# Last head set of four query chunks moved by DMA into a dense out-projection, gate and up in one bank, and a new order

## The chip, the cores and the metric

One core of one Trainium2 chip runs the whole kernel. The metric is device time in microseconds (us) of one execution; the median of three runs of the kernel before is 820.38 us. TensorE is called PE, VectorE DVE, ScalarE ACT, GpSimd POOL, and SyncE, which issues nearly all DMAs, SP.

## What is computed

A transformer block with modulation on x of 2048 tokens by 640, with 32 heads of 20 columns, and a bilinear gated layer of width 1536. All tensors are bf16.

```python
mod = (_silu(c) @ w_mod).reshape(c.shape[0], 6, 1, -1)      # sa, ca, ga, sb, cb, gb
h = _layernorm(x) * (1 + ca) + sa
qkv = (h @ wqkv).reshape(B, S, 3, H, Dh)                    # q, k, v
p = softmax(einsum('bhqd,bhkd->bhqk', q, k) * Dh ** -0.5)
x = x + ga * (einsum('bhqk,bhkd->bhqd', p, v) @ wo)         # attention
h = _layernorm(x) * (1 + cb) + sb
x = x + gb * (((h @ w_gate) * (h @ w_up)) @ w_down)         # bilinear layer, no activation
```

## The kernel before, in words

**Tiles.** Queries are cut into five chunks (CHUNKS): three of 512 and two of 256. The 32 heads are eight head sets of four; the four heads of a set sit in the four 32-row groups of PE. A chunk and a head set make an item, 40 items in all. An item of 512 queries has 64 units: one unit is one head, one tile of 128 keys and 512 queries, a score tile of 128 x 512 in one PSUM bank. In the chunks of 256 queries one unit holds two key tiles, so those items have 32 units. All items together have 2048 units.

**Scores and exp.** A score matmul (L1396) writes a unit. Most units go to ACT, whose exp (L1432) takes two banks at once (1024 columns) into the buffers PP; from score group HEADG on, every second group has three banks (1536 columns), and G, the pool of PSUM banks for other work, then has one bank less. QUADS gives, for each item, how many quads of four units go to DVE instead: DVE computes the exponential in integer arithmetic, with four L1456 (PSUM to DB, 128 x 512) and one each of L1488, L1496 and L1493 (128 x 2048) into two DSS terms. PV (L1922) multiplies PP or DSS by V and adds up in PSUM bank 7.

**End of an item.** DVE transposes the sums (L1576), takes the reciprocal of the denominators (L1579), POOL multiplies (L1581; DVE for the last item), and DVE transposes back into OcT (L1588). For head sets 0 to 6, SP then moves the 20 rows of each head from OcT to their place in Ocp (L1599), which holds the chunk's attention output, transposed, in five blocks of 128 rows. The eighth head set stays in OcT.

**Suffix of a chunk.** `suffix(ci)` projects out: five matmuls of Ocp with wo, and a sixth of OcT with wo7 (the rows of wo of the last head set, laid out as OcT has them). The fifth block of Ocp and of wo therefore holds 48 rows, and zeros behind them. DVE adds the result to xck (L1666), takes statistics (L1676), normalises (L1683); PE transposes (L1694), DVE or ACT evict with the modulation to h2T (L1699, L1701); gate and up (L1769, L1780) give hprod, the down-projection is added to xck (L1803) and goes out (L1812). In chunks 0 to 3 the suffix runs during the next chunk's exps, packed as four column tiles (line L856, `quarters`); a pack that is late may be cut into two halves. The last chunk's suffix runs after the last exp, with whole matmuls (L852, `full`). Weights of gate and up come by DMA into stg, or stx in the last chunk.

**Order.** The order of every engine is written when the program is built. `Sched` is a planner with assumed durations: each task has an engine, dependencies and a priority, and PE's next work is chosen by `pick_pe` from scores, PV and the other rounds (`pick_x`). `gate(w)` holds back a suffix's rounds until a given score group, from GATE_F; PVMIN, PVMAX, PVTOL, D_RES, K_LEAD and the like steer the choice. STEAL_GAP says when ACT may take an eviction from DVE. `do_fill` puts filler matmuls (L2240, L2242) where PE's recent work is low. On the chip each engine runs its list in order and waits on semaphores, so an instruction that waits holds up all behind it.

```python
pcs = oc_pieces(j) if j < NSET - 1 else []
...
mms.append((C320, f))                                   # five of Ocp with wo
f = qf(320, lambda tl=tl: OcT[:, oc_last[ci]["s"], tl * 128:(tl + 1) * 128],
             lambda hf=hf: wo7[:, 320 * hf:320 * hf + 320], False, True)
```

Of the kernel before, what the change touches and what calls it, by code (L numbers as in the profile page):

```python
# [25 lines left out]
DMA_SLOW = 0.0015  # L26
DMA_LAT = 1700.0
STEAL_END = 66197.894
STEAL_GAP = 19.496
HAM_W = 3413.3  # L30
HAM_MIN = 2550.0

# [395 lines left out]
    return nwait  # L428


CHUNKS = [(0, 512), (512, 512), (1024, 512), (1536, 256), (1792, 256)]
QUADS = [(0, 4, 3, 3, 4, 3, 4, 3), (3, 4, 3, 4, 3, 3, 4, 4), (3, 4, 3, 4, 3, 4, 3, 4), (1, 2, 1, 2, 1, 1, 1, 1), 1]
D_LEAD = 0.384
NB0, NSS = 2, 3
HEADG = 600
EAGER = 7
X_POOL, X_PIECES, POOL_NS = 0, 4, 1.95
X_LAST = 2
X_TAIL = 0
XBACK = 1  # L440
HOLD = 110
PVTOL = 245
XDPRIO = 2.0
TPRIO = 0.75
TAHEAD = 1
GU_ONE = 0
XCONT = 0
T3_POOL = 1
HEAD_OUT = 2
NPS = 4  # L450
TS_4X, TT_2X = 600.0, 1145.0
WM_GATE = 9
WM_NEED = 1.798
K_DIRECT = (0, 1, 2, 3)
Q_DIRECT = 2
K_LEAD = 0.686
K_ALL = (0,)
KD_LEAD = 0.409
DMA_WINDOW = 900000
D_LATE = 16  # L460
D_RES = 79
PVMIN, PVMAX, PVCAP = 3, 9, 14
PV0 = 0
V_PARTS = [[0, 4], [4, 8]]
V_L1 = 0.2
# [7 lines left out]
PREEMPT = 0.0  # L473
PRE_M = 0.3
PV0N = 1
GATE_F = [1.0, 0.869, 0.999, 0.673, 1.0]
FILL_MIN = 4200.0
FILL_HARD = 0.0
FILL_T0, FILL_TH, FILL_MINH = 2300.0, 17000.0, 7500.0
FILL_MODE = 'P'  # L480
# [2 lines left out]
LN_POOL = ()  # L483
LN_ACT = [1, 3, 5, 7]
XFIRST = 0
LN2P = 1.775
NALT = 1
OPFIRST = 0
HT_L = 0.11
V_L = 0.208  # L490
LATE_A = 3
LATE_L = 2.394
LATEQ = (3,)
LATEQ_A = 4
LATEQ_F = 0.672
QUAD_GAIN = 0.597233983857778
NTERM = 2
XHALF = 1
X_LATE = 30.0
X_HALF = 0.0  # L500


def ps_cost(n):
    return n * 1.042 + 67.0
# [6 lines left out]
def build_kernel(nc, A_x, A_wqkv, A_wo, B_x, B_w_gate, B_w_up, B_w_down, c, w_mod, out):  # L511
# [852 lines left out]
    for i, (tc, b) in enumerate(ql):  # L1364
        packed_round("Q", b, tc, 500 + i, int(gstart[1] + LATEQ_A + gpc[1] * LATEQ_F * i / len(ql)), True)

    z_wo = pool(630, lambda e: e.memset(wo_sb[:, KD - 1, :], 0.0), t_xn[1], prio=8)
    z_w7 = pool(630, lambda e: e.memset(wo7[:], 0.0), t_xn[1], prio=8)
    d_wo = [dma("sp", 128 * (KD - 1) * D * 2, lambda e: e.dma_start(wo_sb[:, 0:KD - 1, :], wov[:, 0:KD - 1, :]), [d_wm[3][0]],
            prio=10),  # L1370
            dma("sp", 48 * D * 2, lambda e: e.dma_start(wo_sb[0:48, KD - 1, :], wov[0:48, KD - 1, :]), [z_wo, d_wm[4][0]], prio=10.1)]
    d_w7 = [dma("sp", DH * D * 2, lambda e, s=s: e.dma_start(
        wo7[32 * s + 1:32 * s + 1 + DH, :], wov[48 + DH * s:48 + DH * s + DH, KD - 1, :]), [z_w7, d_wm[4][0]], prio=10.2) for s in range(4)]
    t_wo = []
# [192 lines left out]
    oc_free = {}  # L1567
    oc_last = {}

    def item_end_tasks(it):  # L1570
        ci, j = items[it]
        n = CHUNKS[ci][1]
        nb32 = n // 32
        slot = ci % 2
        cell = {}
        t1 = Task("dve", n * 1.1 + 70, lambda e: e.transpose(OT[:, 0:n], ps[:, BPV, 0:n]), [], prio=0.0, name=f"T1.{it}")  # L1576
        t1.acq = [(sOT, "o", 1)]
        item_info[it]["t1"] = t1
        t2 = dve(155, lambda e: e.reciprocal(invT[:, 0:nb32].unsqueeze(2),  # L1579
                                            OT[:, 0:n].rearrange("p (b c) -> p b c", c=32)[:, :, 0:1]), [t1], prio=1.5)  # L1580
        f3 = lambda e: e.tensor_tensor(  # L1581
            OTn[:, 0:n].rearrange("p (b c) -> p b c", c=32), OT[:, 0:n].rearrange("p (b c) -> p b c", c=32),
            invT[:, 0:nb32].unsqueeze(2).to_broadcast([128, nb32, 32]), ALU.mult)
        if T3_POOL and it < len(items) - 1:
            t3 = pool(n * 2.2 + 200, f3, [t2], prio=0)
        else:
            t3 = dvl(sb_cost(n, 1.04), f3, [t2], prio=1.5)
        t4 = dve(n * 1.1 + 65, lambda e: e.transpose(OcT[:, cell["s"], 0:n], OTn[:, 0:n]), [t3], prio=1.5)  # L1588
        pcs = oc_pieces(j) if j < NSET - 1 else []
        t4.acq = [(sOcT, "s", max(1, len(pcs)))]  # L1590

        def on4(task):
            cell["s"] = task.slots["s"]
            sOT.done(0, task)
        t4.on_start = on4
        dms = []
        for (b5, s, r0, nr, ro) in pcs:
            def f(e, b5=b5, s=s, r0=r0, nr=nr, ro=ro):
                return e.dma_start(Ocp[r0:r0 + nr, slot, b5, 0:n],  # L1599
                                   OcT[32 * s + 1 + ro:32 * s + 1 + ro + nr, cell["s"], 0:n])  # L1600
            dps = [t4] + ([z_oc[slot]] if b5 == KD - 1 else [])
            if ci >= 2:
                dps += oc_free[ci - 2]
            else:
                dps += [x for l in tr_last.values() for x in l]
            t = dma("sp", nr * n * 2, f, dps, prio=2, dur=720.0)
            t.on_start = lambda task: sOcT.done(cell["s"], task)
            dms.append(t)
        oc_ready.setdefault(ci, []).extend(dms)
        if j == NSET - 1:  # L1610
            oc_ready[ci].append(t4)
            oc_last[ci] = cell
        sc.left += 1
        t1.seq = 0
        return t1
# [5 lines left out]
    def suffix(ci):  # L1621
# [31 lines left out]
        for tl in range(ntl):  # L1653
            ev = []
            for hf in range(2):
                mms = []
                for k in range(KD):
                    f = qf(320, lambda k=k, tl=tl: Ocp[:, slot, k, tl * 128:(tl + 1) * 128],
                                 lambda k=k, hf=hf: wo_sb[:, k, 320 * hf:320 * hf + 320], k == 0, False)
                    mms.append((C320, f))  # L1660
                f = qf(320, lambda tl=tl: OcT[:, oc_last[ci]["s"], tl * 128:(tl + 1) * 128],
                             lambda hf=hf: wo7[:, 320 * hf:320 * hf + 320], False, True)
                mms.append((C320, f))

                def after(r, tl=tl, hf=hf):
                    f = lambda e: e.tensor_tensor(xck[:, tl, 320 * hf:320 * hf + 320], ps[:, r.b["b"], 0:320],  # L1666
                                                  xck[:, tl, 320 * hf:320 * hf + 320], ALU.add)
                    return [dve(ps_cost(320), f, [r.last, d_xc], prio=1)]
                r = Round(mms, list(oc_ready[ci]) + t_wo + [d_xc], after, pr(True), gate=gate(KD * 320),
                          name=f"op{ci}.{tl}")  # L1670
                ev.append(r.evac[0])
                op_last.append(r.last)
            t = t0 + tl
            bn = []
            for hf in range(2):
                bn.append(dve(ps_cost(320), lambda e, tl=tl, hf=hf: e.bn_stats(  # L1676
                    st2[:, tl, 6 * hf:6 * hf + 6], xck[:, tl, 320 * hf:320 * hf + 320]), [ev[hf]], prio=LN2P))
            ag = dve(115, lambda e, t=t, tl=tl: e.bn_aggr(mv2[:, t, :], st2[:, tl, :]), bn, prio=LN2P)
            f1 = lambda e, t=t: e.tensor_scalar(sd2[:, t:t + 1], mv2[:, t, 1:2], EPS, None, op0=ALU.add)
            p1 = dve(75, f1, [ag], prio=LN2P) if tail else pool(220, f1, [ag], prio=1)  # L1680
            p2 = pool(570, lambda e, t=t: e.tensor_tensor(rs2[:, t:t + 1], sd2[:, t:t + 1], mhalf[:, 0:1], ALU.pow),
                      [p1], prio=1)
            t_xn2.append(dvl(360, lambda e, t=t, tl=tl: e.tensor_scalar(  # L1683
                xn2[:, tl, :], xck[:, tl, :], mv2[:, t, 0:1], rs2[:, t:t + 1], op0=ALU.subtract, op1=ALU.mult),
                [p2] + first, prio=LN2P))
            x1_done += ev
        oc_free[ci] = op_last[-1:]
        op_last[-1].on_start = lambda task: sOcT.done(oc_last[ci]["s"], task)
        t_h2 = []
        tr_l = []  # L1690
        for k in range(KD):
            mms = []
            for tl in range(ntl):
                f = lambda e, b, tl=tl, k=k: e.transpose(bankh(b)[:, tl * 128:(tl + 1) * 128],  # L1694
                                                         xn2[:, tl, k * 128:(k + 1) * 128], ident[:])
                mms.append((C128, f))

            def after(r, k=k):
                f = lambda e: e.tensor_scalar(h2T[:, k, 0:n], bankh(r.b["b"])[:, 0:n], mcol[:, 3, k:k + 1],  # L1699
                                              mcol[:, 2, k:k + 1], op0=ALU.mult, op1=ALU.add)  # L1700
                fa = lambda e: e.activation(h2T[:, k, 0:n], bankh(r.b["b"])[:, 0:n], AFT.Identity,  # L1701
                                            bias=mcol[:, 2, k:k + 1], scale=mcol[:, 3, k:k + 1])
                return [evac(n, n * .78 + 55, f, fa, [r.last, r_sb.evac[0], r_cb.evac[0]] +
                             (first if alt else bd.get("h2T", []) + kv_last))]
            r = Round(mms, list(t_xn2), after, pr(True), gate=gate(n), name=f"h2T{ci}.{k}")
            t_h2.append(r.evac[0])
            tr_l.append(r.last)
# [313 lines left out]
    def pick_x(t, warm=False):  # L2021
# [3 lines left out]
        if xcur[0] is not None:  # L2025
# [3 lines left out]
                a = cand.acq[0][0].avail()  # L2029
                blocked = a is None or a[0] > t  # L2030
            pre = False
            if blocked and len(xstack) < 1 or PREEMPT > t and len(xstack) < 2:
                for task in rl:
                    if not blocked and task.prio >= cand.prio - PRE_M:
                        break
# [282 lines left out]
```

The softmax here doesn't subtract the row's maximum and nothing guards it: scores larger than these inputs give would overflow.

## Time and profile before

| | |
|---|---|
| median of three runs | 820.38 us (820.32 to 820.39) |
| the profiled execution: span | 818.5 us; its own time is not listed apart |
| median above the span | 1.9 us |
| first exp starts, last exp ends | 16.27 us, 784.61 us |
| ACT, PE, DVE, POOL busy | 776.9, 789.8, 717.9, 75.7 us |
| exps | 691 of 1024 columns, 91 of 1536, one of 512 |
| quads on DVE | 98 |

The page gives, for each engine, its busy time and share of the span, then groups of instructions: line, engine, operation, what it writes and reads, the count, after the first bar the busy time in us and the mean of one in ns, after the second the idle time of the engine just before them and the line that ended it. Records of one engine may overlap, so that count times mean can be above busy time. In order of time a row gives start, length, engine, line, operation, tiles and count, and in brackets the idle time before it with what ended it. PEld is the loading of weights, SPq the issue of a DMA by SP.

### The profile page before, as it was taken

To read this page: it belongs to the slowest core of one execution; us is meant where nothing else is said; L and a number is where in the kernel's file an instruction comes from. 1 tells how busy PE (TensorE), PEld (TensorE's weight loads), DVE (VectorE), ACT (ScalarE), POOL (GpSimd) and SP (SyncE) were. 2 spreads that over 40 slices of the span, in tenths; PEclk is the share of its full clock that TensorE was granted. 3 is DMA by queue.
4 is the path that set the end of the run, shared out by engine and by line. 5 is a ranking of instruction groups with operands and counts; after the bars stand their busy time and mean duration, and the time that the engine had idled before them with its cause. 6 is when DMAs were issued, how large, how long until landed. Compare 5 with 4: busy or idle time off the path is not lost.

```text
span 818.5 us, 29494 instructions
## 1 busy us (share of the span) xinstructions
PE 789.8 (96%) x12785; PEld 312.7 (38%) x12785; DVE 717.9 (88%) x1262; ACT 776.9 (95%) x825; POOL 75.7 (9%) x105
## 2 busy tenths in 40 slices
PE   8999999999999999999999999999899999999998
PEld 4433333322232332333333333243254443554567
DVE  7989999999999999999999999999798876658663
ACT  7889999999999999999999999999999999999941
POOL 3300000000012000000011000000020000011000
DMA  9724211114400222400300222000301237124420
GB/s 295 219 79 101 71 45 36 51 52 133 104 16 24 59 65 58 134 13 21 93 3 5 54 54 54 6 14 23 90 5 22 54 80 138 33 75 102 104 52 17
DMA packets 115902, 54.35 MB, mean 66 GB/s; under 512 B 83771, under 2 KB 115775, under 8 KB 115775
## 3 DMA queue, kind: packets, MB, share of 16 engines
q1 hardware_dynamic: 114847, 51.33, 24.4%
q8 instruction: 101, 1.65, 0.8%
q10 hardware_dynamic: 928, 1.15, 0.4%
q14 instruction: 26, 0.21, 0.1%
HBM read 41.75 MB, written 8.41 MB: 61 GB/s over the span
## 4 chain that ended last, share of the span: by engine, by line
ACT 49%; PE 38%; issue 9%; DVE 4%; POOL 0%; ACTq 0%
ACT PP L1432 49%; PE ps_all L1396 11%; PE ps_all L856 11%; PE ps_all L1922 8%; PE ps_all L852 3%; PE ps_all L1116 1%; PE ps_all L1052 1%; DVE DB L1456 1%; PE ps_all L1013 1%; DVE DSS L1493 0%; PE ps_all L877 0%; DVE DSS L1488 0%; DVE DSS L1496 0%; DVE st L957 0%; PE ps_all L2242 0%
## 5 line engine op out<-in xcount | busy, mean ns | idle before, releaser
L1432 ACT ACTIVATE PP<-ps_all 128x1024 bf16<-128x1024 f32 (+1 forms) x783 | 758.4, 1234 | 6.1 <-PE ps_all L1396 3.5
L1396 PE MATMUL ps_all<-QT,KT 32*128 32x512 bf16 (+1 forms) x2560 | 308.3, 340 | 19.6 <-ACT PP L1432 14.8
L1456 DVE TENSOR_SCALAR DB<-ps_all 128x512 int16<-128x512 f32 x392 | 260.5, 683 | 35.5 <-PE ps_all L1396 33.7
L1396 PEld LDWEIGHTS ps_all<-QT,KT 32*128 32x128 bf16 x2560 | 81.4, 92 | 262.9 <-ACT PP L1432 240.9
L1922 PE MATMUL ps_all<-PP,Vf 128*32 128x512 bf16 (+2 forms) x2096 | 165.6, 343 | 0.3 <-DVE OT L1576 0.3
L1493 DVE TENSOR_TENSOR DSS<-DB,DSS 128x2048 bf16<-128x2048 bf16 x98 | 119.2, 1216 | 0.0
L856 PE MATMUL ps_all<-h2T,stg 128*32 128x512 bf16 (+1 forms) x1804 | 117.2, 338 | 0.9 <-DVE DB L1456 0.6
L1581 POOL TENSOR_TENSOR OTn<-OT,invT 128x512 bf16<-128x512 f32 (+1 forms) x39 | 41.6, 1066 | 617.6 <-DVE invT L1579 611.8
L1922 PEld LDWEIGHTS ps_all<-PP,Vf 128*32 128x32 bf16 (+1 forms) x2096 | 47.3, 94 | 86.1 <-issue 78.8
L1922 PE MATMUL ps_all<-DSS,Vf 128*32 128x512 bf16 (+3 forms) x928 | 76.9, 351 | 0.1
L1488 DVE TENSOR_SCALAR DSS<-DB 128x2048 int16<-128x2048 int16 x98 | 68.0, 694 | 1.0
L1496 DVE TENSOR_SCALAR DSS<-DB 128x2048 int16<-128x2048 int16 x98 | 67.5, 689 | 1.1 <-PE ps_all L1922 1.1
L856 PE MATMUL ps_all<-wd,hprod 128*32 128x320 bf16 (+1 forms) x1384 | 58.8, 278 | 0.3 <-DVE xck L1803 0.3
L856 PEld LDWEIGHTS ps_all<-h2T,stg 128*32 128x32 bf16 x1804 | 40.7, 96 | 35.0 <-issue 18.1
L856 PEld LDWEIGHTS ps_all<-wd,hprod 128*32 128x32 bf16 x1384 | 31.5, 96 | 17.7 <-issue 9.1
L1769 DVE CAST gsb<-ps_all 128x512 bf16<-128x512 f32 (+1 forms) x48 | 29.6, 618 | 5.1 <-PE ps_all L856 4.8
L1576 DVE STREAM_TRANSPOSE OT<-ps_all 128x512 f32<-128x512 f32 (+1 forms) x40 | 24.2, 605 | 10.2 <-PE ps_all L1922 10.1
L1922 PEld LDWEIGHTS ps_all<-DSS,Vf 128*32 128x32 bf16 (+1 forms) x928 | 23.5, 95 | 23.4 <-issue 9.1
L1116 PE MATMUL ps_all<-hT,wq 128*32 128x512 bf16 x375 | 31.7, 382 | 0.0
L856 PE MATMUL ps_all<-wV,hT 128*32 128x320 bf16 (+1 forms) x688 | 31.2, 292 | 0.0
L856 PE MATMUL ps_all<-wo,Ocp 128*32 128x320 bf16 (+1 forms) x632 | 30.2, 285 | 0.3 <-DVE xck L1666 0.2
L1780 DVE TENSOR_TENSOR hprod<-ps_all,gsb 128x512 bf16<-128x512 f32 x36 | 24.6, 683 | 2.9 <-PE ps_all L856 2.9
(123 smaller groups left out, 532.9 us busy)
## 6 DMA issues: line engine op xcount, KB each, us to landing
stg<-in_B_w_gate_dram SPq DMA_DIRECT2D x50, 160.0 KB
stg<-in_B_w_up_dram SPq DMA_DIRECT2D x50, 160.0 KB
QT<-q_rows SPq DMA_DIRECT2D x22, 128.0 KB
KT<-k_rows SPq DMA_DIRECT2D x84, 32.0 KB
wm<-in_w_mod_dram SPq DMA_DIRECT2D x3, 800.0 KB
x<-in_A_x_dram SPq DMA_DIRECT2D x7, 320.0 KB
xck<-in_A_x_dram SPq DMA_DIRECT2D x3, 640.0 KB
wd<-in_B_w_down_dram SPq DMA_DIRECT2D x1, 1920.0 KB
```

The source lines that it names most:

```text
L856: return lambda e, b: e.matmul(ps[32 * x:32 * x + 32, b, c0 + o:c0 + o + w], lhs()[:, 32 * x:32 * x + 32], rhs() if w == n else rhs()[:, o ...
L1116: f = [lambda e, b_, k=k, x=x: e.matmul(ps[x:x + min(32, w - x), b_, :], wx[:, k, r0 + x:r0 + min(x + 32, w)], hT[tc][:, k, :], tile_posit ...
L1396: ems.append(lambda e, i=i, kt=kt: e.matmul(dstf()[:, i * u.n:(i + 1) * u.n], KT[32 * u.s:32 * u.s + 32, u.j, kt * 128:(kt + 1) * 128], QT ...
L1432: return e.activation(PPs[g % 2][:, cellp["p"], 0:nu * 512], ps[:, b0:b0 + nu, :].rearrange("p b c -> p (b c)"), AFT.Exp, scale=ESCALE)
L1456: return e.tensor_scalar(DB0[:, st_["slot"], x * 512:(x + 1) * 512], bank(cell["b"]), EBIAS, 0.0, op0=ALU.add, op1=ALU.max)
L1488: return e.tensor_scalar(DSS[:, st_["ss"][0], :], DB0[:, st_["slot"], :], 0x7F, 0x3F00, op0=ALU.bitwise_and, op1=ALU.bitwise_or)
L1493: return e.tensor_tensor(d, DB0[:, st_["slot"], :].bitcast(BF16), d, ALU.mult)
L1496: return e.tensor_scalar(DSS[:, st_["ss"][1], :], DB0[:, st_["slot"], :], 0x7F80, 2, op0=ALU.bitwise_and, op1=ALU.bitwise_or)
L1581: f3 = lambda e: e.tensor_tensor(OTn[:, 0:n].rearrange("p (b c) -> p b c", c=32), OT[:, 0:n].rearrange("p (b c) -> p b c", c=32), invT[:, ...
L1769: f = lambda e: e.tensor_copy(gsb[:, gs, 0:n], ps[:, r.b["b"], 0:n])
L1780: f = lambda e: e.tensor_tensor(hprod[:, fc, 0:n], ps[:, r.b["b"], 0:n], gsb[:, gs, 0:n], ALU.mult)
L1922: ems.append(lambda e, i=i, kt=kt, stt=stt, stp=stp: e.matmul(ps[32 * s:32 * s + mc, BPV, 0:u.n], Vf[:, (kt * H + 4 * u.j + s) * VW:(kt * ...
```

## The change

- For the last head set of chunks 0 to 3, OcT is moved by DMA into the fifth block of Ocp like the others; wo is loaded whole in one DMA, and the out-projection of these chunks has five matmuls. The last chunk keeps OcT and wo7; POOL clears its fifth block of Ocp first (z_tail).
- GU_ONE = 1: in chunks of 256 queries gate and up of one 128-column block share a PSUM bank and one round.
- In the last chunk OP_EARLY lets the five Ocp matmuls start before OcT is there, the sixth being a task of its own; T_SPLIT transposes and evicts h2T by tiles of 128 tokens; TAIL_PRE lets a waiting round be passed over once all scores are issued; EV_OP and LN2T are priorities there.
- QUADS, HEADG and the planner's constants are set anew. GU_OUTER is defined and not used.

```diff
-STEAL_GAP = 19.496
+STEAL_GAP = 184.697
...
-QUADS = [(0, 4, 3, 3, 4, 3, 4, 3), (3, 4, 3, 4, 3, 3, 4, 4), (3, 4, 3, 4, 3, 4, 3, 4), (1, 2, 1, 2, 1, 1, 1, 1), 1]
-D_LEAD = 0.384
+QUADS = ((0, 4, 3, 3, 4, 3, 4, 3),
+         (3, 4, 3, 4, 3, 3, 4, 4),
+         (3, 3, 4, 4, 3, 4, 4, 4),
+         (1, 2, 1, 2, 1, 1, 1, 2),
+         (1, 1, 1, 1, 0, 1, 1, 1))
+D_LEAD = 0.383
...
-HEADG = 600
+HEADG = 580
+OP_EARLY = 1
+EV_OP = 0.5
+T_SPLIT = 1
+GU_OUTER = 4
+TAIL_PRE = 1
+LN2T = 0.6
...
-PVTOL = 245
-XDPRIO = 2.0
+PVTOL = 253
+XDPRIO = 2.163
...
-GU_ONE = 0
+GU_ONE = 1
...
-K_LEAD = 0.686
+K_LEAD = 0.705
...
-KD_LEAD = 0.409
+KD_LEAD = 0.216
...
-D_RES = 79
-PVMIN, PVMAX, PVCAP = 3, 9, 14
+D_RES = 58
+PVMIN, PVMAX, PVCAP = 4, 14, 13
...
-GATE_F = [1.0, 0.869, 0.999, 0.673, 1.0]
+GATE_F = (0.925, 0.688, 1.105, 0.744, 1.0)
...
-LN2P = 1.775
+LN2P = 2.447
...
-LATE_A = 3
-LATE_L = 2.394
+LATE_A = 4.5
+LATE_L = 2.493
...
-X_LATE = 30.0
+X_LATE = -0.231
...
-    z_wo = pool(630, lambda e: e.memset(wo_sb[:, KD - 1, :], 0.0), t_xn[1], prio=8)
...
-    d_wo = [dma("sp", 128 * (KD - 1) * D * 2, lambda e: e.dma_start(wo_sb[:, 0:KD - 1, :], wov[:, 0:KD - 1, :]), [d_wm[3][0]],
-            prio=10),
-            dma("sp", 48 * D * 2, lambda e: e.dma_start(wo_sb[0:48, KD - 1, :], wov[0:48, KD - 1, :]), [z_wo, d_wm[4][0]], prio=10.1)]
+    d_wo = [dma("sp", 128 * KD * D * 2, lambda e: e.dma_start(wo_sb[:, :, :], wov[:, :, :]), [d_wm[3][0]], prio=10)]
...
+        if ci == NC - 1 and j == 0:
+            z_tail[ci] = [pool(1200, lambda e: e.memset(Ocp[:, ci % 2, KD - 1, :], 0.0), list(oc_free[ci - 2]), prio=9)]
...
-        pcs = oc_pieces(j) if j < NSET - 1 else []
+        direct = j == NSET - 1 and ci == NC - 1
+        pcs = [] if direct else oc_pieces(j)
...
-        if j == NSET - 1:
+        if direct:
+            oc_ready[ci] += z_tail[ci]
             oc_ready[ci].append(t4)
             oc_last[ci] = cell
...
-                                 lambda k=k, hf=hf: wo_sb[:, k, 320 * hf:320 * hf + 320], k == 0, False)
+                                 lambda k=k, hf=hf: wo_sb[:, k, 320 * hf:320 * hf + 320], k == 0, k == KD - 1 and not tail)
                     mms.append((C320, f))
...
+                fx = qf(320, lambda tl=tl: OcT[:, oc_last[ci]["s"], tl * 128:(tl + 1) * 128],
+                              lambda hf=hf: wo7[:, 320 * hf:320 * hf + 320], False, True)
+                if tail and not OP_EARLY:
+                    mms.append((C320, fx))
...
+                    if tail and OP_EARLY:
+                        fs_ = fx if isinstance(fx, list) else [fx]
+                        r.last = sc.add(Task("pe", C320, [lambda e, g_=g_: g_(e, r.b["b"]) for g_ in fs_], [r.last, oc_ready[ci][-1]],
+                                             ctr="pex", prio=pq - 1000, name=f"op{ci}.{tl}", mode=r.last.mode))
+                    return [dve(ps_cost(320), f, [r.last, d_xc], prio=EV_OP if tail else 1)]
...
+            if tail and T_SPLIT:
+                pq = pr(True)
+                for tl in range(ntl):
+                    def after(r, k=k, tl=tl):
+                        sl = slice(tl * 128, tl * 128 + 128)
...
+                        return [evac(128, 128 * .78 + 55, f, fa, [r.last, r_sb.evac[0], r_cb.evac[0]] + first, prio=.5 + .01 * k)]
+                    r = Round(mms[tl:tl + 1], [t_xn2[tl]], after, pq + .01 * tl, name=f"h2T{ci}.{k}")
...
-            if blocked and len(xstack) < 1 or PREEMPT > t and len(xstack) < 2:
+            if blocked and len(xstack) < 1 or (PREEMPT > t or TAIL_PRE and pvstate["sidx"] >= NG) and len(xstack) < 2:
```

## The prediction

> **What bounds the kernel now.** I read the page first (part 1, then the largest groups of part 5), then ScalarE alone in order of time, then all engines in order of time over the last 35 us.
>
> ```profile
> PE 789.8 (96%) x12785; PEld 312.7 (38%) x12785; DVE 717.9 (88%) x1262; ACT 776.9 (95%) x825; POOL 75.7 (9%) x105
> ...
> L1432 ACT ACTIVATE PP<-ps_all 128x1024 bf16<-128x1024 f32 (+1 forms) x783 | 758.4, 1234 | 6.1 <-PE ps_all L1396 3.5
> L1456 DVE TENSOR_SCALAR DB<-ps_all 128x512 int16<-128x512 f32 x392 | 260.5, 683 | 35.5 <-PE ps_all L1396 33.7
> ...
> L1493 DVE TENSOR_TENSOR DSS<-DB,DSS 128x2048 bf16<-128x2048 bf16 x98 | 119.2, 1216 | 0.0
> ```
>
> Two engines look full. PE's 96% is not decisive: its records overlap, and it runs fillers (L2242, 304 records). ScalarE decides, because its exps (L1432) lack work for only 6.1 us. ScalarE alone shows where:
>
> ```profile
> 57.33 3.78 ACT L1432 ACTIVATE PP<-ps_all 128x1024 bf16<-128x1024 f32 x4 [1.12 <-PE ps_all L1922]
> 61.82 89.28 ACT L1432 ACTIVATE PP<-ps_all 128x1024 bf16<-128x1024 f32 x97 [0.71 <-PE ps_all L1396]
> 152.11 2.86 ACT L1432 ACTIVATE PP<-ps_all 128x1024 bf16<-128x1024 f32 x3 [1.01 <-PE ps_all L1922]
> 155.14 1.02 ACT L1432 ACTIVATE PP<-ps_all 128x1024 bf16<-128x1024 f32 x1 [0.17 <-PE ps_all L1922]
> 156.55 484.19 ACT L1432 ACTIVATE PP<-ps_all 128x1024 bf16<-128x1024 f32 x515 [0.39 <-PE ps_all L1396]
> 640.92 143.69 ACT L1432 ACTIVATE PP<-ps_all 128x1536 bf16<-128x1536 f32 x127 [0.19 <-PE ps_all L1922]
> ```
>
> From 62 to 784.6 us ScalarE stands idle 1.8 us in all (1.01 + 0.17 + 0.39 + 0.19). So the time is three pieces: the start up to 62 us, the exps, and a tail of 34 us after the last exp, in which PE and VectorE alternate:
>
> ```profile
> 784.76 0.40 PE L1922 MATMUL ps_all<-PP,Vf 128*32 128x256 bf16 x8
> 784.98 2.49 PE L856 MATMUL ps_all<-wd,hprodt 128*32 128x320 bf16 x68
> 787.40 0.85 PE L852 MATMUL ps_all<-wo,Ocp 128*128 128x320 bf16 x5
> 788.09 0.30 PE L852 MATMUL ps_all<-wo,OcT 128*128 128x320 bf16 x1
> ...
> 790.76 3.44 PE L856 MATMUL ps_all<-wd,hprodt 128*32 128x320 bf16 x96
> 794.14 0.73 PE L1694 MATMUL ps_all<-ident,xn2c 128*128 128x128 bf16 x10
> 795.99 1.27 PE L852 MATMUL ps_all<-h2Tc,stx 128*128 128x256 bf16 x10 [1.12 <-ACT h2Tc L1701]
> ```
>
> The last PV ends at 785.16; gate and up of the last chunk start 10.83 us later and run without a gap to the end.
>
> **What the Trainium skill says.** "Perfetto Trace Analysis" (Identifying the Most-Contended Engine) says that matmul busy share is no good measure for TensorE, because matmuls are pipelined, and that the busy share of weight loads is better, while occupancy is fair for ScalarE. The trace agrees: PE is 96% busy with fillers in it, its weight loads 38%. "VectorE: DVE Perf Modes" (perf-mode tier table) gives, for 2048 bf16 elements in SBUF, 693 ns for tensor_scalar and 1224 for tensor_tensor; the rows here say 694, 689 and 1216. "DMA: Bandwidth & Descriptors" (Latency and other measured facts) speaks of a fixed cost of some 2 us; here the K read that waits for its write (SP, L1162 at 151.08 to L1175 at 152.81) puts issue to landing at 1.73 us.
>
> **The change, part by part.** Counts come from both kernels' instruction listings.
>
> 1. Exps. QUADS moves four-unit groups from ScalarE to VectorE: 24, 28, 28, 10, 8 by chunk become 24, 28, 29, 11, 7, so 98 become 99. HEADG 580 instead of 600 makes more exps 1536 wide. Counts: 691 of 1024, 91 of 1536, one of 512 become 679, 98, none. A 1024 slot: (89.28 - 0.27 overlap of the last)/97 = 0.918 us. The last run holds 63 of each width and the 512: (143.42 - 63 x 0.918 - 0.48)/63 = 1.351; 0.43 per 512 columns. Before 634.1 + 122.9 + 0.5 = 757.5; after 623.1 + 132.4 = 755.5. **-2.0 us**, on the path, as ScalarE is full. Stealing (STEAL_GAP) changes no count on ScalarE before the tail.
>
> 2. The extra quad costs VectorE 4 x 0.683 + 0.694 + 0.689 + 1.216 = 5.3 us. It falls in chunk 2, with another in chunk 3 and one less in chunk 4. VectorE was 158.5 of 170 us busy from 425 to 595; plus 5.3 is 96%, the level of 205 to 390 us (178.7 of 185), where ScalarE is full. The listing ends chunk 2's items at the same score counts as before (last item 1547 units against 1546). **0**, covered by ScalarE; bound 0 to +2.
>
> 3. Dense out-projection. For chunks 0 to 3 the sixth matmul (wo<-OcT, 156 records, 10.7 us by record, some 5 us of real PE time) goes; half-width packs also fall. PE is relieved by 5 to 7 us, but it is not the bound: **0** (bound -1.5, if the 1.8 us of stalls in the middle go). In exchange SP issues 16 more DMAs, 0.71 us each, and PE's first out-projection of a chunk waits for their landing. Behind it in PE's order stand score matmuls, so a late DMA idles ScalarE. Price: PV end to OcT end is 5.8, 6.9 and 3.2 us for chunks 0 to 2 (L1576 and L1588 in order of time); three further issues 2.2 and landing 1.7 make 9.7, 10.8 and 7.1. The listing puts the first out-projection 35, 35 and 29 score units after the last PV (before: 17, 22, 18). A unit is 768.3/2048 = 0.375 us, so it stands 13.1, 13.1 and 10.9 us behind. The margins are 3.4, 2.3 and 3.8 us; chunk 3 has 108 units. **0**, bound 0 to +5 over three places. The buffer that held the last head set through the out-projection comes free sooner; no wait for it shows, so 0. wo comes in one DMA instead of two, one POOL memset (0.63) goes and one (0.52) comes: hidden, POOL is 9% busy.
>
> 4. Gate and up in one bank concerns chunks 3 and 4. PE's stream is the same; one eviction now waits for both halves. In chunk 3 other work covers it. In the tail the last product lands 0.37 + 0.42 + waits = about 1.0 us after the last gate/up matmul, but the down-projection takes that block 11 matmuls (1.5 us) after it starts. **0**, bound 0 to +0.5.
>
> 5. Order. PE's listing is the same up to score unit 108, past 62 us, but for one V round cut differently, so the start and its gaps stay: **0**. In the middle new constants reorder projections and gates; I take the same 1.8 us of stalls (0 to 4).
>
> 6. Tail, from the last PV to gate/up (10.83 before). OP_EARLY, T_SPLIT and TAIL_PRE put 13 + 2 Ocp matmuls, 4 OcT, 36 down-projection packs and 10 transposes there; before 20, 4, 41 and 10. PE: 19 x 0.140 (3.37 for 24) + 36 x 0.143 (3.44 for 24) + 0.73 = 8.5, with mode changes about 9.5. VectorE: OcT ends near +1.7 (an xckt add leaves the chain), four adds from +2.3 (0.42 apart, the fourth at +3.6), then bn_stats, first rs at about +6.1, xn2 of tile 0 at +7.2, two h2T evictions, xn2 of tile 1 at +8.9 (it was +8.7: the split evictions go ahead of it), transposes, three evictions of 128 columns. Those are not in the trace: 256 columns take 0.40 on VectorE with 0.32 between starts, 512 take 0.54, so I take 0.26 apart; ScalarE's were 0.46 apart at 256 columns, which bounds its two from above; free evictions would bound from below. Gate/up starts near +10.4. **-0.4 us** (-1.2 if PE's 9.5 binds, +0.6 if evictions of 128 columns cost as much as of 256).
>
> Sum: -2.0 - 0.4 = -2.4. The span goes from 818.5 to 816.1; the median before, 820.38, lies 1.9 above the span, and I keep that: **818.0 us**.
>
> **Rivals.** (a) Better: the reordering also removes the stalls of 1.8 us, and PE alone limits the tail (-1.2). For it: PE has 5 us less to do. Against: the stalls come from order, not amount. 820.4 - 2.0 - 1.5 - 1.0 = 815.9. (b) VectorE becomes the bound in chunk 2: 96% of a stage leaves it little, a late quad holds up PV, PP buffers stay taken, ScalarE waits 2 us: about 820.2, no change. Against: from 205 to 390 us it runs so. (c) Slower, one mechanism: the out-projection reaches the head of PE's queue before its DMAs land. Place: its first matmul in chunks 0 to 2. With 1.5 us of stall at each, 4.5 in all, 820.4 - 2.4 + 4.5 = 822.5; it decides from 4.0 us in all, that is from landings 3 to 5 us later than reckoned. For it: SP is in order and also carries weight loads of 0.5 us. Against: in the waits of the kernel before, PE's weight loads wait for a DMA twice, 2.0 us together, both for wm; no K, Q or weight-tile transfer is among them. (d) That the change does not do what it says: the counts exclude it.
>
> **How the numbers follow.** Forecast 0.55 (own range 817.0 to 819.2), (a) 0.20, (b) 0.14, (c) 0.11. About what a measurement can tell is 0.2%, 1.6 us: faster is below 818.7, slower above 822.0. Of the forecast nine tenths lie below 818.7: 0.50 + 0.20 = 0.70 faster; the rest and (b) 0.19 the same; (c) 0.11. The range 815.9 to 821.2 leaves out half of (a) and most of (c).
>
> **What would show it.** ScalarE full from 62 to about 782.5 us; exps 679 and 98 at 0.918 and 1.351; no wait of L862/L866 wo matmuls for a DMA; gate/up some 10.4 us after the last PV and 22.5 us from there to the end. Exps ending at 784 or later, with gaps that PE or a DMA released, would make it wrong.

## The result, and the profile after

| | before | after |
|---|---|---|
| median of five runs | 820.37 us (820.32 to 820.39) | 817.24 us (816.77 to 818.24) |
| ratio after/before | | 0.9963, 95% interval 0.9953 to 0.9974 |
| profiled execution: time, span | not listed, 818.5 | 816.77, 815.0 |
| first exp starts, last exp ends | 16.27, 784.61 | 16.30, 782.43 |
| last PV ends to gate/up of the last chunk | 10.83 | 9.63 |
| from there to the end | 22.5 | 22.5 |

The kernel after is 3.1 us (0.4%) faster by the medians, and the whole interval of the ratio lies below 1. Its profiled execution is the fastest of its runs, so the parts below add up to 3.5 us of span: 2.2 up to the end of the exps, 1.3 between the last exp and gate/up. The page of the kernel after, part 1 and the exps on ScalarE and VectorE:

```profile
PE 787.8 (97%) x12581; PEld 306.3 (38%) x12581; DVE 722.7 (89%) x1272; ACT 775.9 (95%) x821; POOL 73.3 (9%) x105
...
L1439 ACT ACTIVATE PP<-ps_all 128x1024 bf16<-128x1024 f32 (+1 forms) x777 | 756.9, 1202 | 5.4 <-PE ps_all L1403 3.9
...
L1463 DVE TENSOR_SCALAR DB<-ps_all 128x512 int16<-128x512 f32 x396 | 263.1, 682 | 35.4 <-PE ps_all L1403 34.2
```

VectorE has 99 quads (396/4), and it is busy 4.8 us longer (5.3 were reckoned for one more quad, but its other work changed too). ScalarE alone in order of time, as before (start, length, engine, line, count, idle time before it and what ended it):

```profile
57.36 3.78 ACT L1439 ACTIVATE PP<-ps_all 128x1024 bf16<-128x1024 f32 x4 [1.12 <-PE ps_all L1957]
61.85 21.19 ACT L1439 ACTIVATE PP<-ps_all 128x1024 bf16<-128x1024 f32 x23 [0.71 <-PE ps_all L1403]
83.51 70.36 ACT L1439 ACTIVATE PP<-ps_all 128x1024 bf16<-128x1024 f32 x76 [0.47 <-PE ps_all L1403]
154.16 628.27 ACT L1439 ACTIVATE PP<-ps_all 128x1024 bf16<-128x1024 f32 x638 [0.29 <-PE ps_all L1403]
```

Up to 62 us nothing changes. From there the visible gaps are 0.47 + 0.29 = 0.8 us, where they were 1.8. The last run, 628 us without a gap, holds 540 exps of 1024 columns and 98 of 1536: 540 x 0.918 + 98 x 1.351 = 628.1, the slots of before.

The gaps are not all of the time that is lost beside the exps. From 62 us on, by these slots and without the 40 exps that come earlier, the exps are worth 651 x 0.918 + 91 x 1.351 + 0.48 = 721.0 us before and 639 x 0.918 + 98 x 1.351 = 719.0 after; from the first start to the last end they took 722.8 and 720.6. So 2.0 of the 2.2 us come from the smaller count, and the loss is nearly what it was, 1.8 us before and 1.6 after. Half of it is now hidden: the 99 exps in the two runs from 61.85 and 83.51 us took 91.6 us instead of 90.9, with no gap inside a run.

All engines after the last exp:

```profile
782.45 0.42 PE L1957 MATMUL ps_all<-PP,Vf 128*32 128x256 bf16 x8
782.81 1.94 PE L862 MATMUL ps_all<-wo,Ocp 128*128 128x320 bf16 x13
784.76 0.58 PE L862 MATMUL ps_all<-wo,OcT 128*128 128x320 bf16 x3
...
786.04 3.99 PE L866 MATMUL ps_all<-wd,hprodt 128*32 128x320 bf16 x112
789.96 0.40 PE L1715 MATMUL ps_all<-ident,xn2c 128*128 128x128 bf16 x4
...
792.50 11.08 PE L862 MATMUL ps_all<-h2Tc,stx 128*128 128x256 bf16 x100 [0.26 <-ACT h2Tc L1733]
```

The Ocp matmuls now run while VectorE is still making OcT, and the down-projection of chunk 3 fills PE until the transposes. Only 0.26 us of waiting is left ahead of gate/up, for ScalarE's last eviction.

One reading is new: the five times of the kernel after spread over 1.5 us, those of before over 0.1.

### The profile page after: what moved, and what is told of

Same layout as the page of the kernel before. It is cut to its first block, busy times and chain, and to the rows that moved or that the text cites. A ratio compares the mean times of both kernels' runs of the same rounds, so it can differ in the third digit from the quotient of the medians.

```text
span 815.0 us, 29082 instructions
## 1 busy us (share of the span) xinstructions
PE 787.8 (97%) x12581; PEld 306.3 (38%) x12581; DVE 722.7 (89%) x1272; ACT 775.9 (95%) x821; POOL 73.3 (9%) x105
## 3 DMA queue, kind: packets, MB, share of 16 engines
q10 hardware_dynamic: 928, 1.15, 0.4%
## 4 chain that ended last, share of the span: by engine, by line
ACT 44%; PE 37%; issue 9%; DVE 9%; DMA 1%; ACTq 0%; DVEq 0%
ACT PP L1439 44%; PE ps_all L1403 11%; PE ps_all L866 10%; PE ps_all L1957 7%; DVE DB L1463 3%; PE ps_all L862 3%; PE ps_all L1126 3%; PE ps_all L1062 2%; DVE DSS L1500 1%; DMA wm<-in_w_mod_dram 1%; DVE DSS L1495 1%; DVE DSS L1503 1%; PE ps_all L1023 1%; PE ps_all L887 0%; DVE st L1696 0%
## 5 line engine op out<-in xcount | busy, mean ns | idle before, releaser
L1403 PE MATMUL ps_all<-QT,KT 32*128 32x512 bf16 (+1 forms) x2560 | 309.0, 340 | 17.4 <-ACT PP L1439 13.5
L1403 PEld LDWEIGHTS ps_all<-QT,KT 32*128 32x128 bf16 x2560 | 81.5, 91 | 262.3 <-ACT PP L1439 232.4
L1500 DVE TENSOR_TENSOR DSS<-DB,DSS 128x2048 bf16<-128x2048 bf16 x99 | 122.0, 1232 | 0.0
L866 PEld LDWEIGHTS ps_all<-wd,hprod 128*32 128x32 bf16 x1364 | 30.7, 96 | 18.4 <-issue 10.4
L1587 DVE STREAM_TRANSPOSE OT<-ps_all 128x512 f32<-128x512 f32 (+1 forms) x40 | 24.2, 604 | 4.3 <-PE ps_all L1957 4.2
L2277 PE MATMUL ps_all<-ident 128*32 128x512 bf16 x308 | 27.3, 383 | 0.3 <-DVE DB L1463 0.2
```

Of the source, the lines that this page charges most:

```text
L866: return lambda e, b: e.matmul(ps[32 * x:32 * x + 32, b, c0 + o:c0 + o + w], lhs()[:, 32 * x:32 * x + 32], rhs() if w == n else rhs()[:, o ...
L1403: ems.append(lambda e, i=i, kt=kt: e.matmul(dstf()[:, i * u.n:(i + 1) * u.n], KT[32 * u.s:32 * u.s + 32, u.j, kt * 128:(kt + 1) * 128], QT ...
L1500: return e.tensor_tensor(d, DB0[:, st_["slot"], :].bitcast(BF16), d, ALU.mult)
L2277: task.emits = [lambda e, x=x: e.matmul(ps[32 * x:32 * x + 32, b_, :].rearrange("p (a b) -> p a b", a=4), ident[:, 32 * x:32 * x + 32], id ...
```

## Experiments

All times are medians of 5 to 15 runs, with the range; the ratio is to the kernel before, run again beside each kernel; "fastest" is the fastest run of a kernel. `a_` kernels are the kernel after with an edit, `b_` kernels the one before. Where a place is named, it comes from the start of VectorE's transpose at the end of each of the 40 items (L1587), lined up between two profiles.

### 1. Where the spread comes from

**a_again**: the kernel after, unchanged.

> The changed kernel once more, as the measure for its three variants on the same chip and to see whether its times spread as they did (816.8 to 818.2 us in five runs, the kernel before 820.3 to 820.4). My theory: same kernel, so 816.8 to 818.2, ScalarE idle about 0.8 us between 62 us and its last exp, gate and up of the last chunk 9.6 us after the last PV. Rival (the first profile was a lucky one, its stalls and its tail with it): ScalarE's stalls back near 1.8 us, or the tail near the forecast 10.4.

817.55 us (816.74 to 818.86), ratio 0.9965 (0.9953 to 0.9977). Its profiled run, 818.40 us, is 1.6 us longer than the first, and all of that comes at two places (item ends, us, and the difference to the first profile):

```
chunk.item    first profile    second profile
0.7              218.60        218.58  (-0.02)
1.0              242.44        243.16  (+0.72)
4.4              745.60        746.29  (+0.69)
4.5              759.05        760.71  (+1.66)
4.7              783.09        784.74  (+1.65)
```

At 231 us, SP's queue in the second profile, then PE and ScalarE:

```profile
225.64 0.75 SPq L1611 DMA_DIRECT2D Ocp<-OcT  x1
226.49 0.89 SPq L1194 DMA_DIRECT2D QT<-q_rows  x2
227.43 2.26 SPq L1611 DMA_DIRECT2D Ocp<-OcT  x3
232.11 0.32 PE L866 MATMUL ps_all<-wo,Ocp 128*32 128x320 bf16 x4 [0.55 <-DMA Ocp<-OcT]
232.79 3.77 ACT L1439 ACTIVATE PP<-ps_all 128x1024 bf16<-128x1024 f32 x4 [0.39 <-PE ps_all L1403]
```

This is chunk 0's last head set on its way into the fifth block. In the first profile SP issued at the same times, and PE's first out-projection matmul stood at

```profile
231.40 0.31 PE L866 MATMUL ps_all<-wo,Ocp 128*32 128x320 bf16 x4
```

without a wait: the DMA had landed by then. The second place is a DMA of gate and up weights:

```profile
758.75 1.17 PE L866 MATMUL ps_all<-h2Tt,stg 128*32 128x256 bf16 x36 [1.00 <-DMA stg<-in_B_w_up_dram]
...
760.31 4.63 ACT L1439 ACTIVATE PP<-ps_all 128x1536 bf16<-128x1536 f32 x4 [0.83 <-PE ps_all L1403]
```

In neither place is the time made up later. The tail was the same (9.62 us).

**a_ocp_swap**: SP's list rearranged, all other lists the same.

```diff
+    for lst in (sched.all, order["sp"]):
+        for ci in range(4):
+            own = [t for t in lst if t.name == f"ls{ci}"]     # Ocp DMAs of the last head set
+            at = next(i for i, t in enumerate(lst) if t is own[0])
+            rest = [t for t in lst if all(t is not o for o in own)]
+            lst[:] = rest[:at] + own + rest[at:]
```

> The changed kernel with one thing moved: in SP's list the four DMAs of chunk 0's last head set follow each other; two QT loads that stood after the first of them come behind the fourth. All other engines' lists are unchanged. In a second profile of the changed kernel PE waited 0.55 us at 232 us for the last of these DMAs before chunk 0's first out-projection, and ScalarE 0.39 behind it; in the first profile this matmul came just in time. My theory (that DMA chain has no margin left, and its landing differs from run to run; a later wait of PE for a weight DMA near 759 us is a second such place): no wait at 232 us, as the fourth DMA lands 1.7 us after 228.5 and PE comes at 231.4; fastest run the same 816.8, median 0.2 to 0.6 us below that of the changed kernel, some spread left. Rival 1 (the spread has other causes, this wait is hidden): median and spread the same. Rival 2 (the QT loads, now 2.2 us later, become the wait): +0.5 to +2.

817.14 us (816.73 to 818.57), ratio 0.9966 (0.9953 to 0.9978). In its profiled run no wait stands at 231 us, and every item end is within 0.04 us of the first profile of the kernel after: moving the two QT loads costs nothing. The median is 0.1 to 0.4 us lower than in the two measurements of the kernel after, less than the intervals tell apart, and two of five runs still lie over 818.

The mean granted clock of TensorE in each run tells two kinds of spread apart. In all eleven runs of the kernel after it is 1.00, so their spread (816.74 to 818.86) is not the clock's. With the swap, which a_swap_bn in part 2 has too, six runs have 1.00 and lie between 816.73 and 817.30, and four have 0.998 and lie between 818.35 and 818.57. So the swap takes the wait away in the run profiled, and the six runs suggest that it takes most of the spread at full clock away; six are few, and the wait at 759 us is not touched by it. The other four fit a stretch at half clock as parts 2 and 3 show it. That the swap brings the median down is not shown.

### 2. The tail

```diff
 a_op_late    -OP_EARLY = 1   +OP_EARLY = 0
 a_no_split   -T_SPLIT = 1    +T_SPLIT = 0
 a_tail_off   both of these, TAIL_PRE = 0, EV_OP = 1, LN2T = 2.447
 a_swap_bn    a_ocp_swap with -LN2T = 0.6   +LN2T = 0.4
```

Up to the tail the engines' lists are those of the kernel after (of a_ocp_swap for the last).

> The changed kernel with OP_EARLY 0 alone: the five Ocp matmuls of a block of the last chunk wait for OcT as the sixth does. My theory (VectorE's chain from OcT to xn2 decides the tail, PE is half a us behind): the first add comes 0.5 to 1 us later, as five matmuls per block (0.7 us) stand between OcT and it, and gate/up with it: +0.7 us. Rival (PE's amount of work decides): the same matmuls fit in elsewhere, +0 to +0.2.

> The changed kernel with T_SPLIT 0 alone: transposes and h2T evictions of the last chunk in pairs of 256 columns after both tiles are normalised. My theory (from the forecast's steps: without the split, xn2 of tile 1 is earlier by the two evictions, 0.5 us, but the 256-column evictions end later, 3 x 0.32 on VectorE after it): gate/up +0.3 us, 0 to +0.6. Rival (the split is what made the tail PE-bound): +1.0.

> The changed kernel with the three tail switches off (OP_EARLY, T_SPLIT, TAIL_PRE 0; EV_OP 1, LN2T 2.447); all engines' order before the tail is that of the changed kernel. My theory (the tail is worth the 1.2 us seen between last PV and gate/up, the rest of the gain is exps and stalls): exps end at the same 782.4, gate/up about 10.8 us after the last PV instead of 9.6, total +1.2 us against the changed kernel. Rival 1 (the tail shrank because the fifth-block move took the eighth head set's work elsewhere, not because of the switches): 0. Rival 2 (the switches cost as much as they give, the forecast's -0.4): +0.4.

> A candidate: the changed kernel with chunk 0's four last DMAs together in SP's list, as in the run before, and LN2T 0.4, so that in the tail the statistics of tile 0 come before the last two adds. Expected: no wait at 232 us; gate/up of the last chunk 9.4 to 9.6 us after the last PV (9.6 in the changed kernel, 0.26 of it waiting for ScalarE's eviction); 816.6 at best, median 816.6 to 817.1. Rival (PE's own work fills the tail, or the last two adds hold up tile 1): tail 9.6 to 10.0, median 817.1 to 817.4.

| | last PV to gate/up | fastest run | median, ratio (interval) |
|---|---|---|---|
| after, a_again | 9.63, 9.62 | 816.77, 816.74 | 817.24, 817.55 |
| a_op_late | 10.34 | 817.60 | 819.05, 0.9981 (0.9974 to 0.9989) |
| a_no_split | 9.87 | 817.06 | 818.32, 0.9974 (0.9963 to 0.9984) |
| a_tail_off | 10.16 | 817.39 | 818.58, 0.9978 (0.9968 to 0.9988) |
| a_swap_bn | 9.59 | 816.77 | 817.30, 0.9966 (0.9954 to 0.9979) |

The medians hold the spread of part 1 and a further loss of 1.5 us near 561 us in the profiles of a_op_late and a_tail_off, where TensorE ran at half clock (last section); the tail itself is read from the profiles, and the fastest runs agree with it to 0.2 us. OP_EARLY alone gives 0.7 and the split 0.25, as expected. With OP_EARLY off, five Ocp matmuls stand between OcT and the first add; all engines of a_op_late:

```profile
784.64 2.35 PE L866 MATMUL ps_all<-wd,hprodt 128*32 128x320 bf16 x64
786.92 0.85 PE L862 MATMUL ps_all<-wo,Ocp 128*128 128x320 bf16 x5
787.61 0.30 PE L862 MATMUL ps_all<-wo,OcT 128*128 128x320 bf16 x1
...
795.16 11.08 PE L862 MATMUL ps_all<-h2Tc,stx 128*128 128x256 bf16 x100 [0.20 <-ACT h2Tc L1733]
```

All switches off costs 0.53, not the 1.2 that my theory said, and less than OP_EARLY off alone: the switches do not add up, and why was not tried. The other 0.67 is there with the switches off. What differs there in the lists is chunk 3's down-projection: 28 packs are left after the last PV (64 + 48 records), where the kernel before had 41 (68 + 96); the rest runs earlier, under the exps. Half of the 0.67 lies ahead of the transposes, which start 8.64 us after the last PV instead of 8.98, and half behind them, where VectorE in the kernel before still has an add of the down-projection to do (L1803) and ScalarE evicts three tiles instead of two. That the down-projection is the cause is argued from lists and traces, not tried. In a_swap_bn xn2 of tile 0 came 0.7 us earlier and that of tile 1 0.2, but gate/up at the same time: no gain.

### 3. What paces the exps

Four kernels change the amount of work of one engine and leave the order of all engines as it is.

```diff
 a_sixth      the fifth block's pack issued twice (output: that block counted twice)
+                    if k == KD - 1 and not tail:
+                        f5 = Halved(f + f)
 a_no_pack, b_no_pack
+                    if k == 3 and not tail:
+                        f5 = Halved()                 # nothing issued
 a_exp_less
+            nu = nu - 1 if g in range(60, 780, 30) else nu
```

> The changed kernel with every out-projection pack of the fifth block issued twice in chunks 0 to 3, in the same order of all engines (that block is counted twice in the output of this kernel): PE's work of before is put back, 28 packs, about 4 us, and nothing else. My theory (PE's amount of work is not the bound): 0 to +0.4 us, ScalarE's idle time from 62 us to its last exp up by no more than that. Rival (the relief of PE is what the dense block brought, and took ScalarE's stalls away): +1 us (the stalls that went) to +4 (all of the packs).

> The changed kernel with one of the five out-projection packs (fourth block, left out of the sum) not issued in chunks 0 to 3: 28 packs, about 4 us of PE, less; same order. Issued twice, the fifth block's packs cost 2.5 us beside the wait at 232 us. Theory 1 (in the changed kernel ScalarE and PE are just in balance at the out-projections, so less PE work gives nothing, as ScalarE has no idle time there): 0 to -0.5. Theory 2 (PE is over the balance there, and ScalarE's exps stretch with it without a gap that the profile shows): -1.5 to -2.5.

> The kernel before with one of the six out-projection packs (fourth block, left out of the sum) not issued in chunks 0 to 3, in its own order: what the dense block saves PE, with no DMA and no constant changed. Theory 1 (the forecast's step 3: in the order of before the relief of PE is worth nothing, and it was the new order that spent it): 0 to -0.5, exps end 784.1 to 784.6. Theory 2 (the relief itself is the gain): -1.5 to -2.5.

> The changed kernel with 24 exps cut by one bank (18 of 1024 columns to 512, 6 of 1536 to 1024, every thirtieth score group from 60 on; those probabilities are left out of what ScalarE computes), the same order on all engines. At 0.43 us a bank ScalarE has 10.4 us less to do, PE and VectorE as much as before. Theory 1, that of the forecast (ScalarE alone is the bound, PE has slack): all of it, -8 to -10.4. Theory 2, after the run with the packs issued twice (PE and ScalarE are both full at the out-projections, elsewhere ScalarE): -4 to -8, the gain lost in the stretches of the out-projection. Theory 3 (PE is full throughout, the order paces all): 0 to -3.

| | work | median (range) | ratio (interval) |
|---|---|---|---|
| a_sixth | PE +28 packs, some 4 us | 820.07 (818.82 to 820.90) | 0.9994 (0.9986 to 1.0003) |
| a_no_pack | PE -28 packs | 817.23 (816.78 to 819.20) | 0.9967 (0.9955 to 0.9980) |
| b_no_pack | PE -28 packs | 820.21 (820.08 to 821.69) | 0.9999 (0.9991 to 1.0007) |
| a_exp_less | ScalarE -10.4 us | 816.15 (814.40 to 817.33) | 0.9942 (0.9928 to 0.9955) |

**a_sixth: my theory fell.** Its profiled run loses 1.50 us in chunk 0's out-projection (0.7 of it the DMA wait of part 1, which it shows too), 1.06 in that of chunk 1, 0.13 in chunk 2, 0.47 in chunk 3. Without the wait that is 2.4 us for 28 packs: 0.10 to 0.13 us for each in chunks 0, 1 and 3, most of the 0.14 that a pack takes, and almost nothing in chunk 2. ScalarE in order of time from 154 us on:

```profile
154.23 78.25 ACT L1439 ACTIVATE PP<-ps_all 128x1024 bf16<-128x1024 f32 x85 [0.29 <-PE ps_all L1403]
232.97 501.38 ACT L1439 ACTIVATE PP<-ps_all 128x1024 bf16<-128x1024 f32 x508 [0.50 <-PE ps_all L1403]
734.52 51.08 ACT L1439 ACTIVATE PP<-ps_all 128x1536 bf16<-128x1536 f32 x45 [0.17 <-PE ps_all L1403]
```

The exps end 3.2 us later in all, but the visible gaps grew by 0.7 us only (0.50 + 0.17). The rest is exps that take longer without a gap. Taking a pack away gave nothing in either kernel: b_no_pack's last item ends 0.17 us earlier, and a_no_pack's items end within 0.2 us of those of after up to item 4.5. So in the order of the kernel after PE stands right at the edge at its out-projections: more costs at once, less gives nothing.

**a_exp_less: theory 1, that all of it comes back, fell.** Of 10.4 us less on ScalarE, 1.1 to 1.4 came back in the median, 2.4 in the fastest run. ScalarE's exps by shape in three stretches (count, after the first bar busy time in us and mean of one in ns). Of the kernel after, 62 to 218, 265 to 585 and 597 to 770 us:

```profile
L1439 ACT ACTIVATE PP<-ps_all 128x1024 bf16<-128x1024 f32 x169 | 155.9, 1076 | 1.6 <-PE ps_all L1403 1.5
...
L1439 ACT ACTIVATE PP<-ps_all 128x1024 bf16<-128x1024 f32 x333 | 308.3, 1223 | 0.0
...
L1439 ACT ACTIVATE PP<-ps_all 128x1024 bf16<-128x1024 f32 x77 | 83.7, 1087 | 0.0
```

Of a_exp_less, the same stretches:

```profile
L1440 ACT ACTIVATE PP<-ps_all 128x1024 bf16<-128x1024 f32 x164 | 152.0, 1058 | 3.0 <-PE ps_all L1403 2.4
...
L1440 ACT ACTIVATE PP<-ps_all 128x1024 bf16<-128x1024 f32 x325 | 302.1, 1095 | 0.9 <-PE ps_all L1403 0.2
...
L1440 ACT ACTIVATE PP<-ps_all 128x1024 bf16<-128x1024 f32 x82 | 85.0, 1057 | 0.0
```

A lone exp of 1024 columns has a record of 1.02 us (below); where exps queue, records overlap and their mean grows. In the first and third stretch of the kernel after the mean is 1.08 and 1.09: each exp starts nearly as its scores arrive. There the cuts bought nothing: between 62 and 218 us five cuts are worth 2.2 us, and item 0.7 ends 0.03 us earlier; between 597 and 770 us item ends gain 0.1. In the second stretch, mean 1.22, this run made up 2.1 us of a delay by the cuts; in a_again, which has no cuts, a delay stayed to the end.

The mean record tells how far the scores are ahead of the exps, not how fast ScalarE goes. From the end of one exp to the end of the next, where that next one has 1024 columns, the kernel after takes 0.927, 0.917 and 0.916 us on the mean in the three stretches. In the third stretch ScalarE is thus at its own slot as in the second, in the first 1% above it. So it runs at its full pace over most of the time; but outside the second stretch the scores have hardly any lead, and a single exp that is made shorter only leaves ScalarE waiting for the next scores.

What would let the scores come sooner is open. The median lies in the range of theory 3, but that PE is full throughout is not shown. VectorE is an unlikely cause: it was busy 313 of 320 us where the cuts paid, and 149 of 156 and 130 of 173 us where they did not. PE's own stream is one candidate. Another is that the scores wait for an exp to free their banks: between 62 and 218 us weight loads of L1403 waited for an exp 143 times, 57 us in all. The cuts were also single exps, 30 score groups apart; that shortening every exp would bring as little is not shown.

The delay that it made up is the wait of part 1 once more, with a sequel. PE and ScalarE of a_exp_less, then PE in windows (window and its length, busy time, records, granted clock, then share and GB/s of DMA):

```profile
232.54 0.32 PE L866 MATMUL ps_all<-wo,Ocp 128*32 128x320 bf16 x4 [1.15 <-DMA Ocp<-OcT]
...
233.22 1.02 ACT L1440 ACTIVATE PP<-ps_all 128x1024 bf16<-128x1024 f32 x1 [0.99 <-PE ps_all L1403]
234.58 1.02 ACT L1440 ACTIVATE PP<-ps_all 128x1024 bf16<-128x1024 f32 x1 [0.33 <-PE ps_all L1403]
```

```profile
232.00:234.00 2.00, 1.46 (x21) 0.82 0.00 0
234.00:236.00 2.00, 2.00 (x17) 0.50 0.00 0
236.00:240.00 4.00, 3.98 (x69) 0.91 0.00 0
```

After 1.15 us of waiting PE ran at half clock for 3.4 us (what the three windows lack to full clock is 0.36 + 1.00 + 0.36 us, twice that is the time at half), and a wait of 1.15 us became a loss of 2.6.

### 4. Parts in the other order

```diff
 b_dense       dense out-projection of chunks 0 to 3, all constants of before, tail as before
 a_quads_old
-         (3, 3, 4, 4, 3, 4, 4, 4),
-         (1, 2, 1, 2, 1, 1, 1, 2),
-         (1, 1, 1, 1, 0, 1, 1, 1))
+         (3, 4, 3, 4, 3, 4, 3, 4),
+         (1, 2, 1, 2, 1, 1, 1, 1),
+         (1, 1, 1, 1, 1, 1, 1, 1))
```

> The kernel before with the dense out-projection of chunks 0 to 3 alone, at the constants of before (tail, QUADS, HEADG, gate and up as before): exps as before, the first out-projection of chunks 0 to 3 comes 32, 36, 29 and 29 score units after the last PV (before 17, 22, 18 and 37; the changed kernel 35, 35, 29 and 108). My theory (worth nothing by itself): 820.3 within 0.8 us, exps end near 784.6, and where the DMA margin is thin some runs lose 0.4 to 1 us. Rival 1 (the relief of PE brings the stalls of 1.0 us): 819.3, with ScalarE idle 0.8 instead of 1.8 us after 62 us. Rival 2 (the forecast's rival c, the out-projection waits for its DMAs): 822 to 825, with PE waiting for DMA Ocp at the first out-projection of chunks 0 to 3.

> The changed kernel with the QUADS of before in chunks 2 to 4 (HEADG 580 kept): 98 quads on VectorE instead of 99, exps 679 of 1024, 99 of 1536 and one of 512; the order differs from chunk 2 on. My theory (an exp slot of 1.351 and one of 0.48 are added on a full ScalarE): +1.8 us. Rival 1 (VectorE had no room, and gives back what ScalarE saves): 0 or faster. Rival 2 (the quads of before fit the new order badly): over +3, with new idle time of ScalarE.

**b_dense**: 823.06 us (823.03 to 824.49), ratio 1.0039 (1.0026 to 1.0051), slower by the amount of rival 2, but not by its mechanism: no matmul of PE waits for DMA Ocp, and two weight loads do, 0.5 us together. ScalarE in order of time:

```profile
455.65 5.64 ACT L1435 ACTIVATE PP<-ps_all 128x1024 bf16<-128x1024 f32 x6 [0.82 <-PE ps_all L1953]
461.69 157.39 ACT L1435 ACTIVATE PP<-ps_all 128x1024 bf16<-128x1024 f32 x163 [0.39 <-PE ps_all L1399]
619.99 20.51 ACT L1435 ACTIVATE PP<-ps_all 128x1024 bf16<-128x1024 f32 x18 [0.91 <-PE ps_all L1953]
```

Two of the three new gaps wait for PV (L1953), which frees the PP buffers. Before the first of them PE's list has 48 gate/up records and no PV of PP between 448.3 and 455.2 us, then twelve such PV in a row: with the dense block the planner put gate/up ahead of PV. Visible stalls grow from 1.8 to 3.7 us, the exps end 2.8 later, and the tail stays at 10.83. The dense block by itself, in a planner tuned for the other kernel, is a loss.

**a_quads_old**: 826.68 us (826.15 to 827.09), ratio 1.0077 (1.0065 to 1.0090). The exps end at 787.06 us, 4.6 later instead of 1.8. Their counts are as expected, so the slots account for 1.8; 1.0 is the wait of part 1, which this profile shows too (0.78 us of PE), and near 640 us there is a gap of 1.27 us of ScalarE after another stretch at half clock. Gate/up starts 14.0 us after the last PV, because 10 gate/up packs and 48 down-projection packs of chunk 3 were left for the tail (40 and 192 records). The run is in line with the price of the slots but does not isolate it, and what one more quad is worth alone stays open.

## Why the prediction was right, and where not

The time forecast was 818.0, measured 817.24, inside the range; the direction held. The largest term, the exps, held, by the count and the slots. The tail was mis-sized, and "PE is not the bound" was too strong. That the median came out so near is in part luck: the profiled span fell by 3.5 us where 2.4 were reckoned, and the spread, which the forecast did not have, put the median 0.5 us above the profiled run.

1. **Exps, -2.0.** The counts were right (679 and 98), and by the slots they are worth 2.0 of the 2.2 us by which the exps end earlier. The reason, "on the path, as ScalarE is full", holds for this change, whose order was planned anew around it. It is not a rule for any cut: cutting five times as much off ScalarE, single exps in an unchanged order, bought 1.1 to 2.4 us (a_exp_less). How much the quad and the wider exps bring each was not tried.
2. **Extra quad, 0.** VectorE's busy time grew by 4.8 us and no wait of ScalarE for it appears. Held, by the profile alone.
3. **Dense out-projection, 0.** In the order of before the relief of PE is worth 0.1 us (b_no_pack), as said. In the order of after PE has no room left: 28 packs put back cost 2.4 us (a_sixth). "PE is not the bound" failed there. The DMA margins failed in chunk 0: 3.4 us were reckoned, none is there. OcT was ready 7.1 us after the last PV (218.5 to 225.6), not 5.8; two QT loads stand among the four DMAs on SP, so the last is issued by 229.7; with 1.73 to land that is 231.4, and PE comes at 231.4. PE's own arrival was reckoned right (13.1 us, measured 12.9). Rival (c) is therefore real at one of its three places, at 0.7 us in some runs, not 4.5. Chunks 1 and 2 showed no such wait, but their margins, reckoned in the same way from the trace, are some 1.1 and 0.7 us, not 2.3 and 3.8.
4. **Gate and up in one bank, 0.** From gate/up to the end 22.5 us, as before. Not tried alone.
5. **Order: the same 1.8 us of stalls.** The visible gaps are 0.8 us, but the time lost beside the exps is 1.6. Held: the stalls did not go, they are in part hidden in longer exps.
6. **Tail, -0.4.** Measured -1.2, the lower end of the bound. The term that was mis-sized is VectorE's stretch from the adds to xn2: tile 0 ended 6.7 us after the last PV, not 7.2, tile 1 8.3, not 8.9; from there to gate/up it took 1.3, not 1.5. PE, reckoned at 9.5, then waited only 0.26. Of the 1.2, 0.5 is the switches; the other 0.7 stays with them off (a_tail_off).

Of the rivals (a), 815.9, was right on the tail (-1.2, with PE almost the limit) and wrong on the stalls, which stayed. Rival (b) did not occur.

## What to carry to other kernels

Gaps of a full engine are not all that it loses. Count its instructions, price each at its slot where they queue, and compare the sum with the time from first to last: here the gaps fell from 1.8 to 0.8 us and the loss only from 1.8 to 1.6. Ask too whether its instructions queue or start as their input arrives; in this kernel the mean record against a lone one told (1.22 and 1.08 against 1.02 us). Two engines in balance must be tested from both sides, more work and less, in an unchanged order; here less of either gave little and more of PE cost over half of its length. For a matmul that waits for a DMA, count every DMA ahead of it in the issuing queue, others' too, up to the landing, and compare with the first place where PE can reach it; a margin of zero shows as run-to-run spread before it shows as a wait.

## What the runs showed of the hardware

- A wait of PE of 1.15 us (a_exp_less) was followed by 3.4 us at a granted clock of 0.50. The Trainium skill ("TensorE: Matmul & The Clock Gate", Part 1: The HAM clock gate) says that a free-running window of some 3.4 us decides the clock, and that it is halved after at least one idle window. The half and the length agree; a whole idle window was not needed here, as PE worked on both sides of the wait. Waits of 0.55 to 0.78 us at the same place (a_again, a_no_split, a_sixth, a_quads_old) left the clock at 1.00. In a_op_late it fell without any such wait: in the windows of 1 us from 561 to 565 us it was 0.70, 0.50, 0.50 and 0.59, again 3.4 us at half, in a stretch where the kernel after, with the same list, ran at 1.00; the longest idle time of PE just before was 0.32 us in both. A free-running window would allow for that; what decides it was not tried.
- The same DMA chain of chunk 0 landed at least 1.1 us apart between profiles. In nine profiles SP issued it in the same order. In four of them PE did not wait and began 2.4 us after the issue of the last DMA; in five it waited 0.55, 0.57, 0.66, 0.78 and 1.15 us, the last of these until 3.57 us after that issue.
